# Two sets of accumulator banks for layer one's second products, and weight conversions at other steps

## The chip, the cores and the metric

One core of a Trainium2 chip runs the whole program. The metric is the time of one execution on the device, in microseconds (us). The kernel before was timed three times: median 1095.24 us (1093.38 to 1097.16). The trace belongs to one further execution of 1095.18 us.

The engines are called PE (TensorE, matrix products; its weight loads are listed as PEld), DVE (VectorE), ACT (ScalarE), POOL (GpSimd) and SP (SyncE, which here only issues DMA transfers). Products are accumulated in PSUM, which has eight banks; one bank holds 512 float32 values per partition. Everything else lies in SBUF.

## The reference

Three parts follow one another: a causal attention with a decay, and two feed-forward layers.

```python
# q, k, v: 4 batches x 8 heads x 576 positions x 64; f: 4 x 8 x 576
scores = q @ k.T / sqrt(64) + cum[:, None] - cum[None, :]   # cum = cumsum(log(clip(f)))
attn   = softmax(causal(scores));  x = (attn @ v) -> 2304 tokens x 512
# layer one, w_in 512 x 2048, w_out 2048 x 512 (float64 handed in)
h = x @ w_in;   g = h * tanh(softplus(h));   x = g @ w_out
# layer two, the same shapes
h = x @ w_in;   g = h * cos(h);              out = g @ w_out
```

## The kernel before

**Three products for one.** Each operand of the feed-forward layers is kept as a high and a low part, and a product is three matmuls (high-high, high-low, low-high). The weights arrive as float64 and are turned into the two parts on the chip by `split_weights` (L85 to L139): in 16 pieces per matrix of 512 KB. A piece is loaded by SP into one of three `raw` buffers (L102, two pieces ahead), then DVE shifts (L121), shifts and merges (L122), ACT scales (L130), DVE merges again (L131), ACT writes the high part (L135) and POOL subtracts to get the low part (L136). The generator does one piece each time it is asked (`next`). DVE's instructions of a piece are ordered behind the latest marked DVE instruction of the main stream (L117 to L119). The four matrices are called w1i, w1o, w2i and w2o below; w2i takes the memory of w1i, w2o that of w1o, chunk by chunk, so a piece can be written only when the products that read the old chunk are done.

**Layer one's first products** (`hidden_units`, L156) run while attention is still at work and in a tail after it. One unit is 12 matmuls into one bank for 128 of the 2048 hidden columns of a tile of 256, 288 or 320 tokens; ACT copies the even units, DVE the odd ones into an `hs` buffer (L167, L169), and SP writes a pair to a DRAM tensor `hd` (L170). The tail alternates between two `h` and two `hx` buffers, four banks in all (`hbank`, L687). During the tail w1o is converted, one piece after every second unit (L756 to L758).

**Layer one's second products and layer two** (`ffn_units`, L173) are one list of steps with a lag of three: step m loads and activates, step m - 3 multiplies. Layer one has five token tiles (list `first`, L683: 256 tokens, then four of 512), 72 steps in all: a step of a 512 tile covers one of the 16 column blocks, a step of the 256 tile two. A step reads `hd` into one of six `hl` buffers (L207), ACT applies Mish in place (L278) and makes the high part gh (L304), DVE the low part gl (L309), and PE adds to the tile's four accumulators (L239), which stand in banks acc0 to acc3 (`abank`, L693) for the whole tile. At the end of a tile `evac` (L254) moves each accumulator out: ACT the high part (L268), DVE the low part (L269), and SP writes both to a DRAM tensor `yd` (L273). The next tile's first matmuls use the same four banks.

Layer two has six tiles of 384 tokens, 16 steps each: `load_x` (L185) reads x from `yd`, 12 matmuls into a bank of `hbank` make h (L151), a chain of ACT and DVE (L281 to L309) makes gh and gl, and 9 matmuls (L247) add to three of acc0 to acc3. The x buffers, and the temporaries e and n, lie in a pool that `open_second` (L747) opens only when every `hl` tile of layer one has been loaded, over the memory of the `hl` pool and of one x pool of the first products.

w2i and w2o are converted at the turns of this list: w2i one piece at each turn once w1o is done, w2o one at each turn from step 60 on (L760 to L765).

The code states dependencies and a written order; the order of instructions on each engine is then chosen at compile time by a list scheduler, which runs its own model of the times and takes the earliest-written instruction that is ready in that model. On the chip each engine keeps that order.

Of the kernel before, what the change touches and what calls it, by code (L numbers as in the profile page):

```python
# [10 lines left out]
F32R = mybir.dt.float32r  # L11
# [19 lines left out]
def f(ap):  # L31
    return ap.bitcast(F32)
# [3 lines left out]
def tile_attention_two_ffn(  # L36
# [14 lines left out]
    NT, DM = out.shape  # L51
    DFF = w1_in.shape[1]
    NP = H // 2
    NK = DM // 128
    NCH = DFF // 256
    NJ = DFF // 128
    TH = 512
    TB = 384
# [82 lines left out]
    def weight(layer, j, nm):  # L141
        while (layer, j // 2, nm) not in converted:
            next(weights)
        return W[layer, j // 2, nm]
# [11 lines left out]
    def hidden_units(tiles, p, hbank, ready):  # L156
        for t0, T in tiles:
# [4 lines left out]
            for j in range(NJ):  # L162
# [7 lines left out]
                    nc.sync.dma_start(out=hd[:, j - 1 : j + 1, t0 : t0 + T], in_=hs)  # L170
                yield j

    def ffn_units(first, second, p, hbank, abank, open_second):  # L173
        tiles = [dict(layer=1, t0=t0, T=T, G=TH // T) for t0, T in first]
        tiles += [dict(layer=2, t0=t0, T=T, G=1) for t0, T in second]
        steps = []
# [5 lines left out]
        n_first = sum(tl["layer"] == 1 for _, tl, *_ in steps)  # L182
        xt, hl, hps, st, gst, acc, p2, loaded = {}, {}, {}, {}, {}, {}, [], set()

        def load_x(ti):  # L185
            if ti >= len(tiles) or ti in xt or tiles[ti]["layer"] == 1:
                return
            T, t0 = tiles[ti]["T"], tiles[ti]["t0"]
            if not p2 and len(loaded) < n_first:
                return  # L190
            if not p2:
                p2.append(open_second())
            t = p2[0].tile([128, 2, NK, TB], F32R, tag="x", name="x")[:, :, :, 0:T]
            nc.sync.dma_start(
                out=f(t).rearrange("p h k t -> p (h k) t"),
                in_=yd[:, :, :, t0 : t0 + T].rearrange("p h k t -> p (h k) t"),
            )
            xt[ti] = (t[:, 0], t[:, 1])

        def load_h(n):  # L200
            if n >= n_first or n in loaded:
                return
            loaded.add(n)
            ti, tl, g, gi, ng = steps[n]
            T, t0 = tl["T"], tl["t0"]
            t = hlp.tile([128, TH], F32, tag="hl", name="hl", bufs=6)
            nc.sync.dma_start(  # L207
                out=t.rearrange("p (j t) -> p j t", t=T), in_=hd[:, g[0] : g[-1] + 1, t0 : t0 + T]
            )
            hl[n] = t  # L210
# [7 lines left out]
        def mm_h(n):  # L218
            ti, tl, g, gi, ng = steps[n]
            if tl["layer"] == 2:  # L220
                hps[n] = hbank()[:, 0 : tl["T"]]
                in_products(hps[n], 2, g[0], *xt[ti])

        def mm_o(n, jj):
            ti, tl, g, gi, ng = steps[n]
            T, G, layer = tl["T"], tl["G"], tl["layer"]
            start = gi == 0 and jj == 0
            end = gi == ng - 1 and jj == G - 1
            if start:
                acc[ti] = [abank(i) for i in range(NK if layer == 1 else T // 128)]  # L230
            j = g[jj]
            wh, wl = weight(layer, j, "o")
            gh, gl = gst[n]
            if layer == 1:
                gs = slice(jj * T, jj * T + T)
                for d in range(NK):
                    dsl = (slice(None), j % 2, slice(128 * d, 128 * d + 128))
                    for i, (a, b) in enumerate(((wh, gh), (wh, gl), (wl, gh))):
                        nc.tensor.matmul(  # L239
                            acc[ti][d][:, 0:T], lhsT=a[dsl], rhs=b[:, gs],  # L240
                            start=(start and i == 0), stop=(end and i == 2),
                        )
            else:
                for m in range(T // 128):
                    ms = slice(128 * m, 128 * m + 128)
                    for i, (a, b) in enumerate(((gh, wh), (gh, wl), (gl, wh))):
                        nc.tensor.matmul(  # L247
                            acc[ti][m], lhsT=a[:, ms], rhs=b[:, j % 2, :],
                            start=(start and i == 0), stop=(end and i == 2),
                        )  # L250
            if end:
                evac(ti, tl)

        def evac(ti, tl):  # L254
            t0, T = tl["t0"], tl["T"]
            stage = lambda dt: p.tile([128, 512], dt, tag="stage", name="stage", bufs=4)
            for m, a in enumerate(acc.pop(ti)):
                if tl["layer"] == 2:
                    ob = stage(F32)
                    if m % 2 == 0:  # L260
                        nc.scalar.activation(out=ob, in_=a, func=AF.Copy, scale=UNSCALE)
                    else:
                        nc.vector.tensor_scalar(out=ob, in0=a, scalar1=UNSCALE, scalar2=None, op0=ALU.mult)
                    nc.sync.dma_start(out=out[t0 + 128 * m : t0 + 128 * m + 128, :], in_=ob)
                    continue
                a = a[:, 0:T]
                yh, yl = stage(F32R)[:, 0:T], stage(F32R)[:, 0:T]
                nc.scalar.activation(out=yh, in_=a, func=AF.Copy, scale=UNSCALE)  # L268
                nc.vector.scalar_tensor_tensor(  # L269
                    out=yl, in0=a, scalar=UNSCALE, in1=f(yh), op0=ALU.mult, op1=ALU.subtract  # L270
                )
                for x, t in ((0, yh), (1, yl)):
                    nc.sync.dma_start(out=yd[:, x, m, t0 : t0 + T], in_=f(t))  # L273
# [18 lines left out]
        def a_mid(n):  # L292
            if n in hps:
                e, t = st[n]
                nc.scalar.activation(out=t, in_=t, func=AF.Sin, scale=TWO_PI)  # L295
# [17 lines left out]
        ok = lambda i: 0 <= i < N  # L313
        for m in range(N + LAG):
            for i in range(m, m + 4):
                load_h(i)
            if ok(m):
                if steps[m][3] == 0:
                    load_x(steps[m][0])
                mm_h(m)  # L320
                activate(m)
            if ok(m - 1):
                a_mid(m - 1)
            if ok(m - 2):
                v_2(m - 2)
            yield ("in", m)
            for jj in range(steps[m - LAG][1]["G"] if ok(m - LAG) else 1):
                if ok(m - LAG):
                    mm_o(m - LAG, jj)
                if jj == 0:  # L330
                    if ok(m):
                        v_1(m)
                    if ok(m - 2):
                        v_3(m - 2)
                yield ("out", m)
            if ok(m) and steps[m][3] >= 1:
                load_x(steps[m][0] + 1)

    def attention_units(p, bank):
# [340 lines left out]
        cums.append(cum)  # L680

    hidden = [(0, 256), (256, S - 256)] + [(b * S + x, S // 2) for b in range(1, B) for x in (0, S // 2)]
    first = [(0, NT % TH)] + [(NT % TH + TH * i, TH) for i in range(NT // TH)]  # L683
    second = [(TB * i, TB) for i in range(NT // TB)]
    banks = dict(n=0)

    def hbank():  # L687
        banks["n"] += 1
        if attention_over and banks["n"] % 2:
            return psx.tile([128, 512], F32, tag="hx", name="hx", bufs=2)  # L690
        return psf.tile([128, 512], F32, tag="h", name="h", bufs=2)

    def abank(i):  # L693
        return psx.tile([128, 512], F32, tag=f"acc{i}", name=f"acc{i}", bufs=1)

    hsp = ctx.enter_context(tc.tile_pool(name="hs", bufs=3))
    xsb = [ExitStack(), ExitStack()]
# [14 lines left out]
    hid = hidden_units(hidden, hsp, hbank, lambda n: done_tokens >= n)  # L712
# [29 lines left out]
    w1p = ctx.enter_context(tc.tile_pool(name="w1", bufs=1))  # L742
    mp = ctx.enter_context(tc.tile_pool(name="ff", bufs=3))
    hl_sb = ExitStack()
    hlp = hl_sb.enter_context(tc.tile_pool(name="hl", bufs=6, side="right"))

    def open_second():  # L747
        hl_sb.close()
        xsb[1].close()
        return ctx.enter_context(tc.tile_pool(name="ff2", bufs=2, side="right"))  # L750

    w1o = split_weights(1, "o", w1p)
    w2i = split_weights(2, "i", w0p)
    w2o = split_weights(2, "o", w1p)
    weights = chain(w1o, w2i, w2o)
    for u, _ in enumerate(hid):  # L756
        if u % 2 == 0:
            next(w1o, None)  # L758
    last = len(first) * NJ - NJ // 2
    for u, (kind, m) in enumerate(ffn_units(first, second, mp, hbank, abank, open_second)):  # L760
        if kind == "out":
            if next(w1o, 1) is not None:
                next(w2i, None)
            if m >= last - NJ + 4:
                next(w2o, None)  # L765


# [27 lines left out]
```

## Time and profile before

| | before |
|---|---|
| median of three runs | 1095.24 us |
| the profiled execution | 1095.18 us |
| its span, first to last instruction | 1093.4 us |
| PE busy | 1044.5 us (96%) |
| DVE / ACT / POOL busy | 583.4 / 546.8 / 207.0 us |
| mean granted PE clock | 0.986 of full speed |

Attention with most of the first products fills the time to about 404 us, the tail of the first products runs to 453.83 us, layer one's second products to 689.37 us, layer two to 1088.53 us; then the last result is written. [...]

### The profile page before, as it was taken

Reading aid. Unit: us, or ns where it says so; the run is one execution under the profiler, and the core shown is the slowest. Engines: PE = TensorE matmul, PEld = TensorE weight load, DVE = VectorE, ACT = ScalarE, POOL = GpSimd, SP = SyncE. Lnnn points to the kernel's source line nnn. Section 1 sums busy time; section 2 is a strip of 40 time slices with the busy share of each in tenths; the row PEclk is TensorE's granted clock in tenths of the full one; section 3 lists DMA queues with packets and bytes.
Section 4 is the critical chain, followed back from the end, with each engine's and each line's share of the span. In section 5 each row is a group of like instructions: output and inputs, shape, how many; then the busy total and the mean of one; then the engine's idle time right before and its main releaser. Section 6 shows DMA issues by size and latency. Waiting matters only on the chain.

```text
span 1093.4 us, 17193 instructions
## 1 busy us (share of the span) xinstructions
PE 1044.5 (96%) x6112; PEld 909.2 (83%) x6112; DVE 583.4 (53%) x1390; ACT 546.8 (50%) x1168; POOL 207.0 (19%) x275
## 2 busy tenths in 40 slices
PE   5899999999999999979899998899999999999998
PEld 4577888888888899867687876799999999999997
DVE  6858445444444436787523268765445454454553
ACT  4666556655554445465544565544334343343433
POOL 6738222221122105433100013200000000000000
PEclk9999999999999999989899999899999999999999
DMA  5756423223221147767645364702001020100000
GB/s 139 190 132 188 115 81 85 66 77 85 81 77 55 56 131 223 240 195 240 198 129 170 100 195 152 269 1 68 20 29 59 1 87 1 59 29 1 30 1 29
DMA packets 118709, 111.55 MB, mean 102 GB/s; under 512 B 66000, under 2 KB 91600, under 8 KB 118624
## 3 DMA queue, kind: packets, MB, share of 16 engines
q1 hardware_dynamic: 118624, 110.46, 33.6%
q8 instruction: 48, 0.79, 0.3%
q14 instruction: 37, 0.30, 0.1%
HBM read 77.32 MB, written 33.10 MB: 101 GB/s over the span
## 4 chain that ended last, share of the span: by engine, by line
PE 75%; issue 6%; DMA 6%; POOL 5%; DVE 4%; ACT 2%; SPq 1%; ACTq 0%; POOLq 0%; DVEq 0%
PE h L151 22%; PE acc L247 18%; PE hx L151 9%; PE acc L239 8%; PE s L458 7%; PE s L583 4%; PE s L558 4%; POOL wol L136 3%; DMA raw<-in_moe_w_in_dram 3%; DMA hl<-hd 2%; PE s L424 1%; POOL wil L136 1%; DVE raw L122 1%; DVE gl L309 1%; DVE raw L121 1%
## 5 line engine op out<-in xcount | busy, mean ns | idle before, releaser
L151 PE MATMUL h<-xb,wih 128*128 128x288 f32 (+2 forms) x904 | 201.1, 312 | 0.8 <-DVE hs L169 0.7
L151 PEld LDWEIGHTS h<-xb,wih 128*128 128x128 f32 x904 | 146.6, 188 | 12.2 <-issue 5.9
L151 PE MATMUL h<-xb,wil 128*128 128x288 f32 (+2 forms) x452 | 134.8, 300 | 0.1
L239 PE MATMUL acc<-gl,woh 128*128 128x512 f32 (+1 forms) x320 | 121.9, 381 | 6.9 <-DVE gl L309 6.8
L239 PE MATMUL acc<-gh,wol 128*128 128x512 f32 (+1 forms) x320 | 120.7, 377 | 0.0
L458 PE MATMUL s<-stk 128*128 128x192 f32 (+7 forms) x384 | 111.1, 418 | 10.0 <-DMA stk<-s 4.1
L239 PE MATMUL acc<-gh,woh 128*128 128x512 f32 (+1 forms) x320 | 106.2, 382 | 12.8 <-DVE stage L269 11.8
L521 POOL TENSOR_SCALAR s<-s,sm 128x448 f32<-128x448 f32 (+5 forms) x144 | 87.2, 618 | 163.9 <-DVE sm L519 135.0
L247 PE MATMUL acc<-wol,gh 128*128 128x512 f32 x288 | 112.7, 391 | 0.0
L247 PE MATMUL acc<-woh,gh 128*128 128x512 f32 x288 | 112.2, 390 | 0.0
L247 PE MATMUL acc<-woh,gl 128*128 128x512 f32 x288 | 111.4, 391 | 0.0
L507 ACT ACTIVATE s<-s,mx 128x448 f32<-128x448 f32 (+5 forms) x144 | 83.5, 581 | 52.4 <-DVE mx L501 47.1
L151 PE MATMUL hx<-x,wih 128*128 128x384 f32 x384 | 100.9, 340 | 5.2 <-DMA x<-yd 5.2
L151 PE MATMUL h<-x,wih 128*128 128x384 f32 x384 | 98.1, 337 | 0.0
L309 DVE TENSOR_TENSOR gl<-hl,gh 128x512 fp32r<-128x512 f32 x72 | 57.5, 802 | 71.7 <-ACT gh L304 71.5
L295 ACT ACTIVATE n<-n 128x384 f32<-128x384 f32 x96 | 50.4, 525 | 89.7 <-DVE n L289 89.5
L136 POOL TENSOR_TENSOR wol<-raw,woh 128x512 fp32r<-128x512 f32 x32 | 49.9, 1562 | 212.3 <-PE acc L239 113.7
L501 DVE CUSTOM_DVE_ANT_0 s<-s,maskt 128x384 f32<-128x384 f32 (+6 forms) x152 | 67.6, 452 | 36.8 <-PE s L458 29.6
L309 DVE TENSOR_TENSOR gl<-e,gh 128x384 fp32r<-128x384 f32 x96 | 55.4, 577 | 59.6 <-ACT gh L304 59.5
L151 PEld LDWEIGHTS h<-xb,wil 128*128 128x128 f32 x452 | 84.7, 188 | 1.2 <-issue 0.5
L458 PEld LDWEIGHTS s<-stk 128*128 128x128 f32 (+1 forms) x384 | 64.2, 198 | 25.4 <-issue 6.8
L239 PEld LDWEIGHTS acc<-gh,woh 128*128 128x128 f32 x320 | 62.5, 196 | 26.6 <-DVE stage L269 13.6
(87 smaller groups left out, 1941.4 us busy)
## 6 DMA issues: line engine op xcount, KB each, us to landing
hl<-hd SPq DMA_DIRECT2D x72, 256.0 KB
raw<-in_moe_w_in_dram SPq DMA_DIRECT2D x32, 512.0 KB
raw<-in_moe_w_out_dram SPq DMA_DIRECT2D x32, 512.0 KB
hd<-hs SPq DMA_DIRECT2D x48, 288.0 KB
x<-yd SPq DMA_DIRECT2D x6, 1536.0 KB
yd<-stage SPq DMA_DIRECT2D x32, 256.0 KB
natk<-in_k_dram SPq DMA_DIRECT2D x32, 144.0 KB
out_dram<-stage SPq DMA_DIRECT2D x18, 256.0 KB
```

What stands on the lines that cost most here:

```text
L136: nc.gpsimd.tensor_tensor(out=lo[sl], in0=f(high), in1=f(hi[sl]), op=ALU.subtract)
L151: nc.tensor.matmul(o, lhsT=a[wsl], rhs=b[:, kk, :], start=(kk == 0 and i == 0), stop=(kk == NK - 1 and i == 2),)
L239: nc.tensor.matmul(acc[ti][d][:, 0:T], lhsT=a[dsl], rhs=b[:, gs], start=(start and i == 0), stop=(end and i == 2),)
L247: nc.tensor.matmul(acc[ti][m], lhsT=a[:, ms], rhs=b[:, j % 2, :], start=(start and i == 0), stop=(end and i == 2),)
L295: nc.scalar.activation(out=t, in_=t, func=AF.Sin, scale=TWO_PI)
L309: marks["v1"] = nc.vector.tensor_tensor(out=gl, in0=st.pop(n)[0], in1=f(gst[n][0]), op=ALU.subtract)
L458: marks["score"] = nc.tensor.matmul(o, lhsT=st.rearrange("p j w s -> p (j w s)")[0:128, at : at + m], rhs=st[0:128, j, 1, c0:c1], start=Tr ...
L501: marks["ttr"] = nc.vector.tensor_tensor_reduce(out=s[rows, c0:c1], in0=o, in1=mk, scale=-1.0, scalar=BIG if prev is None or rows.start el ...
L507: nc.scalar.activation(out=s[:, 0:w], in_=s[:, 0:w], func=AF.Exp, scale=-1.0, bias=mx, accum_out=sm[:, j : j + 1])
L521: nc.gpsimd.tensor_scalar(out=s[:, 0:w], in0=s[:, 0:w], scalar1=sm[:, j : j + 1], scalar2=1.0, op0=ALU.mult, op1=ALU.mult)
L558: nc.tensor.transpose(t[:, 128 * x : 128 * x + 128], ss[j][:, QS[c] : QS[c] + 128], ident)
L583: pair = nc.tensor.matmul(t[64 * j : 64 * j + 64, c0:width], lhsT=vt[jb][:, c, j], rhs=pt[:, j, c, c0:width], start=(c == 0), stop=(c == n ...
```

## The change

Five things are altered. (1) The accumulators of every second tile of layer one come from `hbank` (two `h`, two `hx`) instead of acc0 to acc3; with five tiles these are the second and the fourth. (2) The 256-token tile is third instead of first. (3) w1o is asked for after every unit of the tail, and what is left of it is asked for before the second products; w2i at every third step from step 9 on; w2o at two of three steps from step 61 to 71 and then at every second step. (4) x of layer two has a pool `x2` of its own, opened before the second products over the x pools of the first products; its first load stands in the list at step 36 (half of 72). (5) The `hl` pool is on the other side of SBUF, and the pool of e and n is opened over it at step 72.

```diff
-    def ffn_units(first, second, p, hbank, abank, open_second):
+    def ffn_units(first, second, p, hlp, xp, hbank, abank, open_second):
...
-            if not p2 and len(loaded) < n_first:
-                return
-            if not p2:
-                p2.append(open_second())
-            t = p2[0].tile([128, 2, NK, TB], F32R, tag="x", name="x")[:, :, :, 0:T]
+            t = xp.tile([128, 2, NK, TB], F32R, tag="x", name="x")[:, :, :, 0:T]
...
-                acc[ti] = [abank(i) for i in range(NK if layer == 1 else T // 128)]
+                spare = layer == 1 and (len(first) - ti) % 2 == 0
+                acc[ti] = [hbank() if spare else abank(i) for i in range(NK if layer == 1 else T // 128)]
...
+            if m == n_first and not p2:
+                p2.append(open_second())
+            if m == n_first // 2:
+                load_x(len(first))
             if ok(m):
-                if steps[m][3] == 0:
-                    load_x(steps[m][0])
...
-            if ok(m) and steps[m][3] >= 1:
+            if ok(m) and m >= n_first and steps[m][3] >= 1:
                 load_x(steps[m][0] + 1)
...
-    first = [(0, NT % TH)] + [(NT % TH + TH * i, TH) for i in range(NT // TH)]
+    first = [(0, TH), (TH, TH), (2 * TH, NT % TH)] + [(NT - TH * i, TH) for i in (2, 1)]
...
-    hlp = hl_sb.enter_context(tc.tile_pool(name="hl", bufs=6, side="right"))
+    hlp = hl_sb.enter_context(tc.tile_pool(name="hl", bufs=6))
...
-        xsb[1].close()
-        return ctx.enter_context(tc.tile_pool(name="ff2", bufs=2, side="right"))
+        return ctx.enter_context(tc.tile_pool(name="ff2", bufs=3))
...
-    for u, _ in enumerate(hid):
-        if u % 2 == 0:
-            next(w1o, None)
-    last = len(first) * NJ - NJ // 2
-    for u, (kind, m) in enumerate(ffn_units(first, second, mp, hbank, abank, open_second)):
-        if kind == "out":
-            if next(w1o, 1) is not None:
-                next(w2i, None)
-            if m >= last - NJ + 4:
-                next(w2o, None)
+    for _ in hid:
+        next(w1o, None)
+    for _ in w1o:
+        pass
+    xsb[1].close()
+    xp = ctx.enter_context(tc.tile_pool(name="x2", bufs=2, side="right"))
+    ends = NJ * (len(first) - 1) + NJ // 2
+    for kind, m in ffn_units(first, second, mp, hlp, xp, hbank, abank, open_second):
+        if kind != "out":
+            continue
+        if m >= 8 and m % 3 == 0:
+            next(w2i, None)
+        if m >= ends - NJ + 4 and (m % 3 if m < ends else m % 2):
+            next(w2o, None)
```

## Rows read from the trace of the kernel before

**Rows 1.** Windows by stage: stretch, length, busy (instructions) per engine, clock, DMA, GB/s
```profile
404.00:453.83 49.83, 49.13 (x370) 48.89 (x369) 35.62 (x60) 28.37 (x53) 22.13 (x13) 1.00 0.77 238
453.83:488.48 34.65, 25.85 (x195) 24.71 (x193) 28.11 (x37) 19.37 (x34) 12.63 (x10) 0.92 0.67 210
488.48:542.81 54.33, 48.03 (x192) 36.96 (x192) 35.72 (x49) 32.34 (x58) 15.18 (x11) 0.94 0.69 208
542.81:589.46 46.65, 46.05 (x193) 37.59 (x193) 13.65 (x21) 21.53 (x37) 0.00 (x0) 0.95 0.44 135
589.46:634.01 44.55, 43.83 (x193) 35.95 (x193) 13.64 (x21) 22.06 (x37) 0.00 (x0) 1.00 0.46 142
634.01:689.37 55.36, 46.93 (x193) 36.77 (x193) 40.84 (x55) 30.13 (x51) 17.15 (x12) 0.95 0.62 200
689.37:1088.53 399.16, 399.16 (x2015) 364.12 (x2016) 207.27 (x403) 167.74 (x309) 5.51 (x4) 0.99 0.11 40
```

**Rows 2.** Waits of PE from 440 us on: total us, times, longest us
```profile
PE acc L239 <- DVE stage L269: 11.8, 5, 5.9
PE acc L239 <- DVE gl L309: 6.8, 9, 1.9
PE hx L151 <- DMA x<-yd: 5.2, 1, 5.2
```

**Rows 3.** Timeline of PE in layer one's second products
```profile
453.83 0.28 PE L239 MATMUL acc<-gh,woh 128*128 128x256 f32 x1
...
462.46 0.28 PE L239 MATMUL acc<-gh,woh 128*128 128x256 f32 x1
...
542.81 0.79 PE L239 MATMUL acc<-gh,woh 128*128 128x512 f32 x1 [4.05 <-DVE stage L269]
```

**Rows 4.** Chain of waits in layer two, same step of two tiles: start, us, what
```profile
896.71 2.08 PE h L151 x12
...
962.89 2.08 PE h L151 x12
```

**Rows 5.** Chain of waits at the end of layer one: start, us, what
```profile
680.62 1.38 DVE gl L309
...
682.03 6.88 DMA x<-yd
```

**Rows 6.** Timeline of DVE in the tail of the first products
```profile
425.41 0.41 DVE L121 TENSOR_SCALAR raw<-raw 128x512 int32<-128x512 int32 x1
425.85 0.69 DVE L122 SCALAR_TENSOR_TENSOR raw<-raw 128x512 int32<-128x512 int32 x1
427.36 0.93 DVE L131 SCALAR_TENSOR_TENSOR raw<-raw 128x512 int32<-128x512 int32 x1 [0.81 <-ACT raw L130]
428.20 0.44 DVE L169 COPY hs<-h 128x288 f32<-128x288 f32 x1
428.57 0.41 DVE L121 TENSOR_SCALAR raw<-raw 128x512 int32<-128x512 int32 x1
...
438.48 0.43 DVE L121 TENSOR_SCALAR raw<-raw 128x512 int32<-128x512 int32 x1 [0.35 <-DMA raw<-in_moe_w_out_dram]
...
457.83 0.45 DVE L169 COPY hs<-h 128x288 f32<-128x288 f32 x1
...
458.72 1.84 DVE L122 SCALAR_TENSOR_TENSOR raw<-raw 128x512 int32<-128x512 int32 x1
```

**Rows 7.** Timeline of POOL in the same tail
```profile
432.25 1.81 POOL L136 TENSOR_TENSOR wol<-raw,woh 128x512 fp32r<-128x512 f32 x1 [1.35 <-ACT woh L135]
...
458.69 1.32 POOL L136 TENSOR_TENSOR wol<-raw,woh 128x512 fp32r<-128x512 f32 x1 [1.33 <-ACT woh L135]
```

**Rows 8.** Timeline of SP's queue in the same tail: issue of a load
```profile
434.08 0.33 SPq L102 DMA_DIRECT2D raw<-in_moe_w_out_dram  x1
```

**Rows 9.** Timeline of DVE in the first tile, the fourth and eleventh gl
```profile
463.94 0.69 DVE L309 TENSOR_TENSOR gl<-hl,gh 128x512 fp32r<-128x512 f32 x1
...
491.23 1.81 DVE L309 TENSOR_TENSOR gl<-hl,gh 128x512 fp32r<-128x512 f32 x1
```

## The prediction

> **What bounds the kernel now.** I read the windows cut at the starts of the five tiles of layer one's second product, then TensorE's waits, then its timeline where it waits, then the chain of waits, and last VectorE, GpSimd and SyncE where the weights are converted. In the windows the reader is to see that the two long stretches, the last first products (404 to 453.83) and layer two (689.37 to 1088.53), keep TensorE full, and that all of its idle time after 404 lies between 453.83 and 689.37, with a granted clock of 0.92 to 0.95 in four of the five tiles there [rows 1].
>
> Each tile has a price without loss. Tile 3, the quiet one (no conversion, GpSimd 0.00), has 43.83 us of matmuls [rows 1], and tiles 1, 2 and 4 issue the same 192. The first tile is half as wide: its third step begins at 462.46, 72 matmuls after 453.83, or 0.120 us each, and 192 of them make 23.0 us [rows 3]. Sixteen steps of layer two take 962.89 - 896.71 = 66.18 us [rows 4], six such tiles 397.1. Against the windows [rows 1] the losses are: tile 0 34.65 - 23.0 = 11.6, tile 1 54.33 - 43.8 = 10.5, tile 2 2.8, tile 3 0.7, tile 4 55.36 - 43.8 = 11.5, layer two 399.16 - 397.1 = 2.1. Together 39.2 us. Of these 23.8 are waits: 11.8 for the move of an accumulator out of its bank (the longest 5.9, the second 4.05 at 542.81), 6.8 for a gl, 5.2 for x of layer two [rows 2, 3]. The other 15 us are matmuls at the low clock after such waits.
>
> The profiled execution took 1095.18 us, 1.78 more than its span of 1093.4, and the median of the three runs is 1095.24: no correction. With all 39.2 us gone it would take 1056.0.
>
> **The change part by part.** *Two bank sets.* Tiles 1 and 3 take their four accumulators from the pair of two-buffer tags that layer two's first products use, tiles 0, 2 and 4 keep the old four. With five tiles each neighbour has the other set, so the first matmul of a tile no longer waits for the four moves of the tile before. The 11.8 us go. What is late next is gl: its chain (ACT gh, DVE gl) runs up to two steps ahead of its matmuls, about 5.4 us. After the quiet boundaries (542.81 on, and in tile 3) no gl wait follows the moves, and I price the moves at nothing there. Tile 4 is on the old set, so layer two's first products find their banks long free; its first second product needs the old set back, but a first product of 12 matmuls (2.08 us [rows 4]) lies between, as at all tiles of layer two, where TensorE never waits [rows 1].
>
> *Tile order.* The half tile goes from first to third. Same 72 steps and 960 matmuls. The first step now takes 2.7 us instead of 2.9 but each pair of steps uses one weight chunk, 5.4 us per chunk in place of 2.9: the weights w1o are needed later. Cost 0, perhaps a little below.
>
> *x of layer two.* Before, its transfer is issued at 682.03, right behind the last gl (680.62 + 1.38), since it lies in memory that the hl tiles still hold, and takes 6.88 us [rows 5]; TensorE stands 5.2 us for it and runs slow after. Now it has its own memory, taken from the x of the last first products, and is issued half way through layer one's steps, more than 30 steps (over 80 us) before it is needed. On SyncE's queue the hl loads behind it may land up to 6.88 us later; there are six hl buffers, so a load goes out some five steps (13 us) before use: hidden. Gain 5.2 + 2.1 in layer two. The memory of e and n is now opened over the hl tiles; the first e may wait for a late gl, with three more steps of 4.8 us before its product is due: 0.
>
> *w2i and w2o.* Before, one piece is asked for at every step's turn, and 16 w2i pieces run through tiles 0 and 1, 10 or so w2o pieces through the end of tile 4, with VectorE at 28.11 of 34.65 us, 35.72 of 54.33 and 40.84 of 55.36, against 13.64 of 44.55 in the quiet tile [rows 1]. Now w2i comes at every third step from step 9: 8.2 us of TensorE for three gl and one piece, well under the load of tile 1. I leave 1 us there (bounds 0 and the 6.8 us of all gl waits before). w2o comes at two steps of three in the last 12 steps: 8 pieces in about 33 us, 0.24 per us. In tile 4 before it is 11 GpSimd subtractions in its last 45 us [rows 1], the same density. There the loss without the x wait and the boundary was 11.5 - 5.2 - 0.7 = 5.6 us; 8/11 of it is 4.1. Bounds 0 and 5.6; I take 3.5, nearer the row, since the ring of raw buffers is what paces it in both.
>
> *w1o.* One piece behind each of the last first products instead of every second. This is the one part that loads a full stretch. VectorE's period there is one hs copy and one piece: first shift at 425.41, shift-and-or at 425.85, the last one from 427.36 after a wait for ScalarE, hs copy at 428.20, next first shift at 428.57: 3.16 us, in which TensorE needs 3.20 (two units of 1.6 us) [rows 6]. A piece costs 428.20 - 425.41 = 2.8 us of this chain, an hs copy 0.37. TensorE has four banks of lead, and VectorE's last hs copy stands at 457.83, 4 us behind TensorE's end at 453.83 [rows 6, 3]: there is no slack left. Best: nothing changes, and a wait of 0.7 us goes. Worst: all 16 pieces lie in front of the first 16 of the tail's 31 units (49.83 / 1.6): 16 x 2.8 + 8 x 0.37 = 47.8 us in place of 25.6, a loss of 22.2. I take one more piece in front of the last hs copy (16 instead of 15), 2.8 us, because pieces can't come denser than the ring of three raw buffers lets them: a load goes out at 434.08, right as GpSimd ends at 432.25 + 1.81 [rows 7, 8]; VectorE waits for it until 438.48, 4.4 us [rows 6]; and with 434.06 - 428.57 = 5.5 us from a first shift to the end of its subtraction [rows 6, 7] that is 9.9 us for three pieces, 3.3 each. And where more is asked for already (two pieces per step in tile 0), the order on VectorE holds seven pieces for eight gl from 463.94 to 491.23 [rows 9]: the order follows the ring and not the demand.
>
> **Sum.** 1056.0 + 2.8 (tail of the first products) + 1.0 (w2i) + 3.5 (w2o) = 1063.3, forecast 1063 us.
>
> **The rivals.** *The stalls only change their name.* The moves at 488 and 542 are late since VectorE and ScalarE are full of pieces; without the bank wait TensorE would stand for gl at the same places. For it: gl waits lie around them, up to 1.9 us [rows 2]. Against it: the pieces leave these places too. Price: half of the 22.1 us lost in tiles 0 and 1 stays, 11 us more: 1074.
>
> *The tail of the first products is ordered by demand.* If the order on VectorE holds more pieces per hs copy than one, TensorE loses 2.8 us for each. At 1.3 pieces it is about 9 us, 1072; at two 22.2 in place of 2.8, 1083. For it: no slack there, and pieces stand earlier in the written order than later hs copies. Against it: the ring, and the order in tile 0.
>
> *Slower: the tail goes by demand and GpSimd blocks VectorE there.* One shift-and-or takes 0.69 us at 425.85, but 1.84 at 458.72, where a GpSimd subtraction (from 458.69) runs beside it [rows 6, 7]. With a piece per 1.6 us unit GpSimd, at 1.3 to 1.8 us a piece, is nearly always at work, and if both two-input operations of a piece waited it out, a piece costs 2.8 + 1.15 + 0.91 = 4.9 us: 16 x 4.9 + 3.0 - 25.6 = 56 us lost, 1116. It makes the kernel slower from 3.8 us a piece on, with all pieces in the first 16 units. [...] Against it: the last step of a piece is GpSimd's own, behind VectorE's, so a chain of pieces partly orders itself: in the dense tile 0 it came to about 3.9 us a piece with the gl in it, and only seven to eight gl [rows 9].
>
> **Chances.** Forecast 0.67, stalls renamed 0.12, tail by demand 0.13, tail by demand with the lock 0.08, of which 0.02 would end within 0.3% (about 3.3 us, what a measurement of this kernel can tell from no change). So faster 0.92, same 0.02, slower 0.06. The range goes from 1055 (all losses gone and the 0.7 us too) to 1083 (two pieces per hs copy): it leaves out the last rival and the tails.
>
> **What would show it.** Right: no wait of TensorE for the move out of an accumulator in layer one; the x transfer issued before 600 us; the first second product near 457 (1 to 4 us late at most); the five tiles in under 205 us; granted clock 0.98 or more in each; layer two at 397. Wrong: waits for gl of a microsecond or more in tiles 0 to 3 (first rival), TensorE waiting for hs copies before the first second product (second), two-input operations of 1.8 us in every piece there (third). A time above 1083 would say that the order of the tail decides and that I misread the ring.

## The result, and the profile after

The changed kernel takes 1082.4 us (median of four runs, 1078.07 to 1084.23) against 1094.55 us for the kernel before beside it: ratio 0.988, 95% interval 0.9844 to 0.9916. It is 12 us faster, where 1063 and so 31 to 32 us were forecast. The profiled execution is the fastest of the four (1078.07 us, span 1076.3); its losses are those of a good run. The program of e8 below turned out to have the same order of instructions and gave 1078.96 (1078.26 to 1079.9), so two sets of runs of one order of instructions can have medians 3 us apart.

The head of the page of the changed kernel, engines only:

```profile
PE 1039.7 (97%) x6112; PEld 902.3 (84%) x6112; DVE 575.3 (53%) x1390; ACT 541.0 (50%) x1168; POOL 200.1 (19%) x275
```

The windows that answer to [rows 1], cut at the last first product (460.34), the starts of the tiles in their new order (506.68, then the half tile at 557.01, 584.13, 628.88) and the end of layer one; columns as there, with the clock that TensorE was granted as a share of full speed:

```profile
404.00:460.34 56.34, 52.25 (x382) 50.22 (x379) 35.75 (x62) 30.24 (x56) 18.73 (x13) 1.00 0.72 227
460.34:506.68 46.34, 45.12 (x195) 35.41 (x193) 21.68 (x30) 21.25 (x38) 8.01 (x6) 1.00 0.56 168
506.68:557.01 50.33, 46.72 (x192) 35.03 (x192) 25.96 (x38) 26.88 (x48) 6.55 (x5) 1.00 0.64 210
557.01:584.13 27.12, 25.41 (x193) 24.81 (x193) 18.68 (x28) 16.20 (x29) 7.12 (x5) 0.94 0.84 287
584.13:628.88 44.75, 44.12 (x194) 35.89 (x193) 19.27 (x28) 24.47 (x47) 4.25 (x3) 1.00 0.56 173
628.88:680.00 51.12, 50.58 (x230) 42.19 (x229) 35.83 (x52) 30.12 (x51) 11.86 (x9) 1.00 0.56 176
```

TensorE's waits from 395 us on, which answer to [rows 2] (total us, times, longest us; `h` and `hx` at L236 are the second set of accumulators, at L151 the banks of first products):

```profile
PE h L151 <- DVE hs L169: 2.7, 4, 1.0
PE acc L236 <- DVE gl L306: 2.3, 4, 1.4
PE hx L236 <- ACT gh L301: 2.1, 3, 1.5
PE hx L236 <- DVE gl L306: 2.0, 5, 0.7
PE hx L151 <- ACT hs L167: 1.4, 2, 1.2
PE acc L236 <- ACT gh L301: 0.9, 3, 0.4
PE acc L244 <- DVE stage L266: 0.7, 1, 0.7
```

The waits that the change was to remove are gone: none in layer one for the move out of a bank (11.8 us before), none for x (5.2 us). In their place stand 7.3 us for gh and gl, and 4.1 us for hs copies where 0.7 stood. Against the prices of the prediction (43.8 us a tile, 23.0 for the half tile), tile 1 in the new order loses 50.33 - 43.8 = 6.5 us, the half tile 4.1, tile 3 0.9. Tail and first tile lie partly over each other; from 404 they should end at 453.83 + 43.8 = 497.6 and end at 506.68, 9.0 us late. About 1.4 of these 9.0 arose before the tail: the first of its 31 units starts at 404.77, against 403.37 in the kernel before. Together that is 20.5 us, and 1.6 are left for the rest up to the 22.1 by which the span of 1076.3 exceeds 1054.2, the span before without its 39.2 us of losses. VectorE, at 25.96 of 50.33 us in tile 1, is not full, nor is ScalarE, at 26.88. Much of what was won is TensorE's clock: the mean granted clock rose from 0.986 to 0.996, and as an estimate (1 - 0.986) x 1093.4 = 15.3 us were lost to it before and (1 - 0.996) x 1076.3 = 4.3 after, 11.0 of the 17.1 us between the two spans.

What ScalarE waits for tells more. The first row is the kernel before, the second the changed one, each its longest total in layer one's stretch (395 to 700 us):

```profile
ACT hl L278 <- DMA hl<-hd: 47.6, 43, 3.5
```

```profile
ACT hl L275 <- DMA hl<-hd: 74.7, 49, 5.2
```

In the changed kernel's timeline of ScalarE the reader is to see that a Mish (L275) stands in front of a gh (L301) and waits; the first time L130, an instruction of a piece, lies between them. A timeline row has start, duration, engine, line, operation and operands, and in square brackets the idle time of the engine before it and what ended it:

```profile
486.55 0.62 ACT L301 ACTIVATE gh<-hl 128x512 fp32r<-128x512 f32 x1
489.99 0.63 ACT L275 ACTIVATE hl<-hl 128x512 f32<-128x512 f32 x1 [2.82 <-DMA hl<-hd]
490.53 0.64 ACT L130 ACTIVATE raw<-raw 128x512 f32<-128x512 f32 x1
491.07 0.62 ACT L301 ACTIVATE gh<-hl 128x512 fp32r<-128x512 f32 x1
...
534.35 0.63 ACT L275 ACTIVATE hl<-hl 128x512 f32<-128x512 f32 x1 [5.18 <-DMA hl<-hd]
534.88 0.61 ACT L301 ACTIVATE gh<-hl 128x512 fp32r<-128x512 f32 x1
```

SyncE's queue in the same stretch: the load that the Mish of 489.99 waits for goes out at 486.01 (the first of the three in that row), behind the reload of a raw buffer; the load that the Mish of 534.35 waits for goes out at 524.90, behind the transfer of x:

```profile
485.47 0.38 SPq L102 DMA_DIRECT2D raw<-in_moe_w_in_dram  x1
486.01 6.82 SPq L203 DMA_DIRECT2D hl<-hd  x3
...
524.26 0.59 SPq L190 DMA_DIRECT2D x<-yd  x1
524.90 3.98 SPq L203 DMA_DIRECT2D hl<-hd  x2
```

VectorE there: the gl that frees the buffer (ends at 485.99), and the gl that comes out at the end of the way round, behind a piece's last merge:

```profile
484.61 1.38 DVE L306 TENSOR_TENSOR gl<-hl,gh 128x512 fp32r<-128x512 f32 x1 [1.36 <-ACT gh L301]
...
491.19 0.69 DVE L131 SCALAR_TENSOR_TENSOR raw<-raw 128x512 int32<-128x512 int32 x1 [2.23 <-ACT raw L130]
491.80 0.68 DVE L306 TENSOR_TENSOR gl<-hl,gh 128x512 fp32r<-128x512 f32 x1
```

And TensorE just after the second wait:

```profile
535.55 0.50 PE L236 MATMUL hx<-gh,woh 128*128 128x512 f32 x1 [1.52 <-ACT gh L301]
```

So there is a way round: gl of a step frees its hl buffer, the load for the step six later goes out, it lands (486.01 to 489.99, 4.0 us), ScalarE's Mish of that far step runs, and only then the gh of a near step. Counting from 0, the rows show gl of step 9, load and Mish of step 15, then gh and gl of step 11. From the end of one gl (485.99) to the end of the other (491.80 + 0.68) that takes 6.5 us. Counted in the compiled order of ScalarE, over steps 8 to 63, a gh has on the mean 4.8 more Mish than gh in front of it (4.9 in the kernel before); "five ahead" below means this count. With six buffers and five ahead, the way round leads from the gl of one step to that of the second step after it, and TensorE takes 5.4 us for two steps. The experiments ask whether it is this order that costs.

### The profile page after: what moved, and what is told of

Read it like the earlier page. It is cut to its first block, busy times and chain, and to the rows that moved or that the text cites. A ratio compares the mean times of both kernels' runs of the same rounds, so it can differ in the third digit from the quotient of the medians.

```text
span 1076.3 us, 17200 instructions
## 1 busy us (share of the span) xinstructions
PE 1039.7 (97%) x6112; PEld 902.3 (84%) x6112; DVE 575.3 (53%) x1390; ACT 541.0 (50%) x1168; POOL 200.1 (19%) x275
## 5 line engine op out<-in xcount | busy, mean ns | idle before, releaser
L151 PE MATMUL h<-xb,wih 128*128 128x288 f32 (+2 forms) x904 | 201.7, 313 | 3.5 <-DVE hs L169 2.7
L151 PEld LDWEIGHTS h<-xb,wih 128*128 128x128 f32 x904 | 146.6, 188 | 15.8 <-issue 5.9
L151 PE MATMUL h<-xb,wil 128*128 128x288 f32 (+2 forms) x452 | 134.8, 300 | 0.1
L306 DVE TENSOR_TENSOR gl<-hl,gh 128x512 fp32r<-128x512 f32 x72 | 63.1, 879 | 71.4 <-ACT gh L301 70.2
L151 PE MATMUL hx<-x,wih 128*128 128x384 f32 x384 | 99.6, 336 | 0.0
L151 PE MATMUL h<-x,wih 128*128 128x384 f32 x384 | 97.7, 336 | 0.0
L306 DVE TENSOR_TENSOR gl<-e,gh 128x384 fp32r<-128x384 f32 x96 | 58.2, 606 | 61.3 <-ACT gh L301 61.2
L151 PEld LDWEIGHTS h<-xb,wil 128*128 128x128 f32 x452 | 84.7, 188 | 1.2 <-issue 0.5
L275 ACT ACTIVATE hl<-hl 128x512 f32<-128x512 f32 x72 | 45.1, 629 | 78.3 <-DMA hl<-hd 74.7
L301 ACT ACTIVATE gh<-e 128x384 fp32r<-128x384 f32 x96 | 50.4, 525 | 58.6 <-DVE e L297 52.8
L136 POOL TENSOR_TENSOR wol<-raw,woh 128x512 fp32r<-128x512 f32 x32 | 43.9, 1375 | 168.6 <-ACT woh L135 164.2
L151 PEld LDWEIGHTS hx<-x,wih 128*128 128x128 f32 x384 | 70.2, 188 | 3.8
L151 PEld LDWEIGHTS h<-x,wih 128*128 128x128 f32 x384 | 70.1, 188 | 3.7
```

Source lines behind the costliest of these rows:

```text
L136: nc.gpsimd.tensor_tensor(out=lo[sl], in0=f(high), in1=f(hi[sl]), op=ALU.subtract)
L151: nc.tensor.matmul(o, lhsT=a[wsl], rhs=b[:, kk, :], start=(kk == 0 and i == 0), stop=(kk == NK - 1 and i == 2),)
L275: nc.scalar.activation(out=e, in_=e, func=AF.Mish, scale=UNSCALE)
L301: nc.scalar.activation(out=gh, in_=e, func=AF.Copy)
L306: marks["v1"] = nc.vector.tensor_tensor(out=gl, in0=st.pop(n)[0], in1=f(gst[n][0]), op=ALU.subtract)
```

## The experiments

All medians are of four to eight runs; the kernel before had 1094.2 to 1094.8 us beside them.

| run | median us | ratio to before | 95% interval |
|---|---|---|---|
| changed kernel | 1082.4 | 0.9880 | 0.9844 to 0.9916 |
| e1_pin | 1062.45 | 0.9706 | 0.9685 to 0.9727 |
| e2_half | 1076.17 | 0.9834 | 0.9815 to 0.9852 |
| e3_pin_half | 1058.81 | 0.9679 | 0.9662 to 0.9696 |
| e4_banks_only | 1090.79 | 0.9967 | 0.9955 to 0.9980 |
| e5_double | 1082.18 | 0.9883 | 0.9860 to 0.9906 |
| e6_pin_double | 1063.64 | 0.9714 | 0.9689 to 0.9739 |
| e7_before_pin | 1077.67 | 0.9849 | 0.9819 to 0.9878 |
| e8_x_late | 1078.96 | 0.9854 | 0.9832 to 0.9876 |
| e9_double_beside | 1071.86 | 0.9787 | 0.9770 to 0.9804 |
| e10_pin_double_beside | 1062.09 | 0.9690 | 0.9670 to 0.9711 |
| e11_before_pin_banks | 1080.74 | 0.9863 | 0.9840 to 0.9886 |
| e12_pin4 | 1062.21 | 0.9710 | 0.9693 to 0.9727 |

**e1: the order of ScalarE alone.** The edge (`issue_after`) adds no work, it only asks the scheduler to put one instruction behind another; the compiled order then has three Mish ahead at each gh of steps 8 to 63. The scheduler also moves some VectorE instructions and DMA issues, so the result is that of the edge with what it brings along.

```diff
+                    if n - 3 in ghs:
+                        hold.enter_context(tc.issue_after(ghs[n - 3].ins))
                     nc.scalar.activation(out=e, in_=e, func=AF.Mish, scale=UNSCALE)
...
-            nc.scalar.activation(out=gh, in_=e, func=AF.Copy)
+            ghs[n] = nc.scalar.activation(out=gh, in_=e, func=AF.Copy)
```

> Changed kernel with one edge more: on ScalarE the Mish of step n stands behind the gh of step n-3. Nothing else is added or left out. Theory A (ScalarE's order): the changed kernel loses some 12 us in the second products since Mish of a step five ahead stands in front of the next gh and waits for an hl load whose buffer has only just come free and that lands behind a weight load; with the edge it finds its load landed. Expected: ScalarE's wait for hl falls from 78 us to under 25, TensorE's waits for gh and gl from 7.3 to under 2, time about 1070 (10 to 14 us under the changed kernel, ratio to before 0.974 to 0.980). Rival B (VectorE and ScalarE are simply full of pieces beside gl): no change, ratio 0.986 to 0.990.

Measured 1062.45, 20 us under the changed kernel by the medians, 16.5 under e8, its repeat, and 15.8 by the spans of the two profiled runs (1076.3 and 1060.5), the changed kernel's being its fastest: 16 to 20 us, more than theory A asked for. The windows of its tiles 1, 2 (half) and 3:

```profile
505.18:548.70 43.52, 43.52 (x194) 36.04 (x192) 23.10 (x37) 26.48 (x48) 7.90 (x6) 1.00 0.76 244
548.70:571.73 23.03, 23.03 (x193) 23.03 (x192) 15.95 (x22) 14.00 (x25) 5.77 (x4) 1.00 0.95 325
571.73:615.28 43.55, 43.55 (x195) 36.06 (x193) 20.64 (x32) 24.63 (x45) 3.98 (x3) 1.00 0.56 177
```

These three tiles have no loss left: the half tile runs at full speed beside DMA engines that are busy 0.95 of the time. TensorE's waits and ScalarE's wait for hl in that run:

```profile
PE h L151 <- DVE hs L169: 3.7, 5, 1.5
PE acc L236 <- DVE gl L309: 0.7, 1, 0.7
```

```profile
ACT hl L278 <- DMA hl<-hd: 7.2, 5, 2.4
```

From 74.7 us to 7.2, and ScalarE now waits for TensorE at gh, with the Mish behind it at once:

```profile
491.84 0.63 ACT L304 ACTIVATE gh<-hl 128x512 fp32r<-128x512 f32 x1 [1.57 <-PE acc L236]
492.37 0.62 ACT L278 ACTIVATE hl<-hl 128x512 f32<-128x512 f32 x1
```

That ScalarE keeps its order also where the instruction in front waits is seen in the changed kernel: the gh of 534.88 (step 25) stood behind a Mish that had waited 5.18 us, while its own Mish had ended at 522.69 and the buffer it writes, one of three, was last read by the matmuls of step 22, which ended at 528.59. Rival B, full engines, is out: the pieces are all still there, and the busy time of VectorE (575.3 and 574.4 us) and ScalarE (541.0 and 542.6) is hardly changed.

**e2: w1o as before.** The tail asks for a piece after every second unit again.

```diff
-    for _ in hid:
-        next(w1o, None)
+    for u, _ in enumerate(hid):
+        if u % 2 == 0:
+            next(w1o, None)
```

> Changed kernel, but a w1o piece is asked for after every second unit of the tail, as before. Theory T (the denser pieces in the tail of the first products cost it 5 to 6 us): the waits for hs copies (4.1 us) go but for 0.7, time 4 to 6 us under the changed kernel, ratio 0.982 to 0.985. Rival (the raw ring paces the pieces whatever is asked, the tail's loss is from elsewhere): within 2 us of the changed kernel.

Measured 1076.17, 6.2 us under the changed kernel. The waits for hs copies fall from 4.1 to 1.1 us, as theory T had it:

```profile
PE h L151 <- DVE hs L169: 0.9, 2, 0.6
PE hx L151 <- ACT hs L167: 0.2, 1, 0.2
```

In the changed kernel VectorE's order has 13 shift-and-merge instructions (L122, one a piece) for the 11 hs copies after the one at 419.36 up to that at 465.17, 1.2 for one; here it is one for one, as in [rows 6]. The size is less sure: the two intervals just overlap. Against e8 it is 2.8 us. In the profiled runs the 31 units of the tail take 53.0 us against 55.9 (50.6 in the kernel before), so 2.8 us are won there, and the spans (1074.5 and 1076.3) differ by 1.8. The waits for gh and gl do not shrink (9.5 us, 7.3 in the changed kernel).

**e3: both.**

> Both: Mish behind the gh of three steps before, and w1o at every second unit. If theories A and T hold and their losses lie in different stretches, they add: 15 to 19 us under the changed kernel, about 1064, ratio 0.969 to 0.975. If only A holds 1070, if neither 1082.

Measured 1058.81, 23.6 us under the changed kernel, more than expected. It is the fastest version here, 35.6 us under the kernel before. Beside the edge the half density is worth 3.6 us (1062.45 to 1058.81), 3.7 by the spans (1060.5 and 1056.8); the two intervals overlap.

**e4: two bank sets alone, in the kernel before.** The edit is the `spare` lines of the change.

> Kernel before with the two bank sets alone (tiles 1 and 3 from the four h and hx banks). Theory: the 11.8 us of waits for the moves go and about half comes back as waits for gl at the same places, as the pieces still fill VectorE and ScalarE there: 5 to 8 us under before, ratio 0.993 to 0.996. Rival (the banks were the whole wait): 12 us and the clock with it, ratio 0.984 or less.

Measured 1090.79: 3.6 us won, less than either asked for. Its waits of TensorE from 440 us on (total, times, longest):

```profile
PE acc L240 <- DVE gl L310: 8.0, 10, 1.4
PE hx L151 <- DMA x<-yd: 6.7, 1, 6.7
PE hx L240 <- DVE gl L310: 6.5, 7, 1.9
```

The waits for moves are gone, those for gl have risen from 6.8 to 14.5 us: the stall has changed its name.

**e5, e6: doubled transfers, first try.**

```diff
+                if (layer, nm) == (2, "i"):
+                    scratch = dram.tile([128, per, 2 * nn], I32, name=f"scratch{i}")
+                    nc.sync.dma_start(out=scratch, in_=src[:, u : u + per])
```

> Changed kernel, and with each raw load of w2i a second transfer of the same 512 KB from DRAM to DRAM on the same queue (16 in all); no engine but SyncE gets anything more to do. Theory A (hl lands behind the weight load, and ScalarE's order lets that late landing hold up the next gh): each of the 16 adds 1 to 2 us before the next hl lands, TensorE loses 10 to 25 us more, ratio to before 0.997 to 1.011, and ScalarE's wait for hl goes from 78 us to over 95. Rival B (engines full of pieces): no change, ratio 0.986 to 0.990.

> The same doubled transfers in the kernel with Mish behind the gh of three steps before. Theory A: the landing has some four steps (11 us) of room, so little is lost: within 3 us of the kernel with the edge alone (1062), ratio 0.970 to 0.974. If the DMA itself were the limit, whatever ScalarE's order: as much is lost as without the edge, 1072 to 1087.

Measured 1082.18 and 1063.64, no change from either base. Both missed their aim: nothing tied the second transfers to the first, and the compile-time scheduler put them into the attention stage.

**e7: the edge in the kernel before.**

> Kernel before with the edge alone (Mish behind the gh of three steps before). Theory A: the same hold-up is part of what tiles 0, 1 and 4 lose in the kernel before, but the bank waits and the x wait stay: 8 to 14 us under before, ratio 0.987 to 0.993. Rival (in the kernel before it is the pieces on VectorE and the banks alone): under 3 us, ratio 0.997 to 1.0.

Measured 1077.67, 16.5 us under the kernel before beside it (1094.19), more than expected. ScalarE's wait for hl falls from 47.6 us to 0.7:

```profile
ACT hl L281 <- DMA hl<-hd: 0.7, 2, 0.4
```

The profiled run is the slowest of the four (1082.06 us). The order held the kernel before up as well: the edge alone, without bank sets, thinner pieces or early x, is worth about as much as the whole change without the edge (the intervals overlap).

**e8: x later.**

```diff
-            if m == n_first // 2:
+            if m == n_first - 6:
```

> Changed kernel with the first load of x of layer two in the list at step 66 instead of 36. Theory A: the 1.5 MB transfer between the hl loads costs the changed kernel 3 to 5 us (ScalarE waited 5.2 us for the hl load behind it, TensorE 1.5, and a low clock later); moved to where no w2i load runs, 2 to 4 us are won, ratio 0.984 to 0.986. Rival: the x transfer is hidden as forecast, within 1.5 us of the changed kernel.

Measured 1078.96, 3.4 us under the changed kernel, but this tests neither theory: the edit did not reach the chip. Only the written order changed. The scheduler issued the load of x at the same place as before, behind the same raw load:

```profile
524.11 0.39 SPq L102 DMA_DIRECT2D raw<-in_moe_w_in_dram  x1
524.67 0.59 SPq L190 DMA_DIRECT2D x<-yd  x1
```

In the two traces the order of instructions of every engine, and of the DMA issues, is the same. So e8 is a repeat of the changed kernel, and 3.4 us is scatter between sets of runs. That the x transfer holds up a Mish and through it a matmul stands in the rows of 524.26, 524.90, 534.35 and 535.55; what a later x would bring was not measured.

**e9, e10: doubled transfers beside the raw loads.** As e5 and e6, with the second transfer ordered behind the first on SyncE:

```diff
+                    with tc.issue_after(ld.ins):
+                        nc.sync.dma_start(out=scratch, in_=src[:, u : u + per])
```

> As the run with doubled transfers, but each of the 16 second transfers (512 KB, DRAM to DRAM) is now queued right behind the raw load that it doubles, in front of the next hl load; in the run before they had all been put into the attention stage, 300 us away from the place in question. Theory A (hl lands behind the weight load, and ScalarE's order lets that hold up the next gh): 10 to 25 us lost against the changed kernel, ratio to before 0.997 to 1.011. Rival B (engines full, the landing is not what holds up gh): ratio 0.986 to 0.991.

> The same transfers beside the raw loads in the kernel with Mish behind the gh of three steps before. Theory A: within 4 us of the kernel with the edge alone (1062.5), ratio 0.970 to 0.975. If the DMA is the limit whatever the order: 10 us or more lost, 0.980 or above.

e9 measured 1071.86: more transfers, and 10.5 us less. Both theories are wrong here as they were put. The compiled order goes with theory A's cause: Mish now stands later, 4.0 ahead on the mean instead of 4.8 (one to three over some stretches), and ScalarE's wait for hl falls from 74.7 to 45.5 us:

```profile
ACT hl L279 <- DMA hl<-hd: 45.5, 35, 8.3
```

That the scheduler's model counted the loads as slower, and so put Mish later, is the likely reason; no run shows it. The same transfers under the edge cost nothing (1062.09 against 1062.45). So under the edge the DMA is not the limit. That a landing behind a raw load lengthens the way round is seen in the changed kernel: from the issue of an hl load to the Mish that waits for it 4.0 us pass at 486.01 and at 494.74, right behind a raw load, and 2.7 to 2.8 at 475.40, 477.44 and 480.14, where no raw load goes out between 468.84 and 485.47; how much of the loss it makes beside the piece's own instructions there was not separated, since every such edit also changes the order.

**e11: edge and banks, without the rest of the change.**

> Kernel before with the edge and the two bank sets. With the edge the bank sets alone should pay what the waits for moves still cost there (5.5 us and the low clock behind): 1069 to 1073, 5 to 9 us under the kernel before with the edge, where without it they paid 3.6. Rival: they pay no more than 4 us here too, since gl is late at the same places.

Measured 1080.74 against 1077.67 without the banks: they pay nothing here, the rival held. Its waits of TensorE:

```profile
PE hx L240 <- DVE gl L313: 5.5, 7, 1.3
PE hx L151 <- DMA x<-yd: 5.3, 1, 5.3
PE acc L240 <- DVE gl L313: 5.1, 4, 2.7
```

What is left in its way is gl on VectorE; in its tile 1, which takes 53.44 us, VectorE with a piece at every turn is busy 39.10. That the pieces make gl late there is read from this, not tested. With edge and the whole change together it is 1062.45 (e1), 15.2 us under e7; how these divide among tile order, thinner pieces, denser w1o, early x and the banks was not measured.

**e12: one step looser.** As e1 with n - 4 in place of n - 3.

> Changed kernel with the edge one step looser: the Mish of step n behind the gh of step n-4. In the trace of the changed kernel the way round (gl, hl load issued, landed, Mish, gh, next gl) takes about 4.3 us without a piece and about 7 with one (1.6 for landing behind the raw load, 1.1 for the piece's own ScalarE and VectorE instructions in between). The order with five ahead gives it two steps, 5.4 us; four ahead three steps, 8.2; three ahead four, 10.9. If that is right, four ahead loses hardly more than three: 1062 to 1066, ratio 0.970 to 0.974. Rival (every step that Mish is early costs alike): half way, 1070 to 1075, ratio 0.977 to 0.982.

Measured 1062.21, no different from three ahead: the bound by steps holds, the rival (each early step costs alike) does not. The order has 4.0 ahead, and ScalarE still waits for hl:

```profile
ACT hl L278 <- DMA hl<-hd: 26.3, 18, 6.0
```

These waits hardly reach TensorE any more: it has one of 0.6 us for gh. Two steps of room are too few in this kernel, three are enough.

## Why the prediction was right and wrong

**Right.** The 39.2 us of losses were nearly all there to be had: e3 has a span of 1056.8, 2.6 us over 1054.2. The bank waits and the x wait went; x was issued at 524.26, before 600; layer two runs at its price; the half tile and the banks in turn cost nothing by themselves, as the e1 windows show. Of the other signs of being right three did not come: the five tiles took 219.7 us (460.34 to 680.00, some 6 of them layer two's first products) and not under 205, the half tile had a clock of 0.94 and not 0.98, and the tail ended at 460.5 and not near 457.

**Luck.** That e1, at 1062.45, lands on the forecast of 1063 is no confirmation. e1 has an edge that the forecast did without, and what it still loses lies elsewhere: tile 1 starts at 505.18 instead of 497.6, 7.6 us late (2.4 of them from before the tail), where 2.8 was forecast, while behind it the 4.5 us put on w2i and w2o are not lost.

**The step that failed** is in the part on x of layer two: "there are six hl buffers, so a load goes out some five steps (13 us) before use: hidden", with the 0 thereby put on hl loads that land late, and the 1 us left for w2i, worked out from the load of VectorE alone. The first use of a load is not its gh but its Mish, and in ScalarE's compiled order the Mish stands five ahead, in front of a near gh. The room was two steps, not five, and a late landing or a piece in the loop could go through to TensorE. That term was 16 to 20 us (e1 against e8 and against the changed kernel) in place of about 1. The trace of the kernel before could have told it: ScalarE's 47.6 us of waits for hl, which the prediction does not use.

**The denser w1o.** Forecast 2.8 us; measured between 1.8 and 6.2 (e2), or 3.6 with the edge, so whether the size was wrong is not settled. The argument that the raw ring alone sets the order was half true: demand doubled, the order took 1.2 pieces for one hs copy. That is the second rival, under its lower price (9 us at 1.3). The tail loses more than this term: 55.9 us for its 31 units against 50.6, of which 2.4 stay with the half density; their cause is open.

**w2o:** forecast 3.5; after tile 3 only 1.6 us are lost in all. Two small misreadings moved nothing: a step of layer two takes 66.18 / 16 = 4.1 us, not 4.8, and the step that begins at 462.46 is the fourth, as the 72 matmuls say.

**The rivals.** The first, stalls that change their name, came nearest: the sign it gave for itself, waits for gl of a microsecond or more in tiles 0 to 3, is in the profile (1.4, and 1.5 for gh), and e4 shows it for the banks alone. Its reason was wrong, since VectorE and ScalarE were not full there and the stall came by ScalarE's order behind the loads. The third, that GpSimd blocks VectorE, did not decide: the tail lost some 5 us and not 56, and of the 31 two-input operations of pieces between 404 and 466 us two took more than 1.6 us, 1.68 and 1.74 (three of 31 between 404 and 460 in the kernel before).

## What to carry to other kernels

Where an engine prepares data far ahead, look at what stands behind the preparation in its compiled order, as the gh of 534.88 stood behind a Mish that had waited 5.18 us: prefetch depth counts from the first instruction that needs the load, not from the one on the critical path (here two steps, 5.4 us, and not five). When waits are removed one by one and time hardly moves, count how many preparations are in front of each critical instruction in the compiled order; an ordering edge that adds no work was worth 16 to 20 us here, with the change and without it. An engine that is busy half the time can still set the pace, as ScalarE did with 26.88 of 50.33 us in tile 1. And before an experiment is read, compare the compiled order with that of its base: e5 and e6 put their transfers elsewhere, e8 changed nothing, and e9 changed more than was meant.

## What was not expected of the hardware

TensorE kept a granted clock of 1.00 through tile 1 of the changed kernel, with five listed waits of 0.2 to 1.5 us and 3.6 us idle in all, and had 0.94 in the half tile behind it (1.7 us idle, one wait of 1.4 us that ended at 568.26; right behind it, from 569.10 to 572, the clock stood at 0.50). In the kernel before, single waits of 5.9 and 4.05 us went with 0.92 to 0.95 over a whole tile [rows 1 to 3]. Yet tile 1 loses 6.5 us with 3.6 us idle and a full clock: a matmul after a wait is shown with 0.50 us in place of 0.39, also after waits too short to be listed. The tile has eleven such restarts. At each the next matmul starts 0.34 us later instead of 0.23, and the last matmul before the gap counts as busy for its full 0.39 us, where in the stream the next one would start after 0.23. As an estimate that is 0.11 + 0.16 = 0.27 us each and 3.0 us together, which covers the other 2.9.
